# Head of stage 0 in a mixer kernel: v first, a fold in 64x64 quarters, four x tiles ahead of the first softmax, float32 work of PE in shared runs, w1's remainders on GpSimd

## The chip, the cores and the metric

The kernel runs on one core of a Trainium2 chip. The metric is the device time of one execution in microseconds (us), and lower is better. Engines are named as in the profile: PE (TensorE matmul), PEld (its weight loads), DVE (VectorE), ACT (ScalarE), POOL (GpSimd), SP (the queue that issues most transfers).

## The reference

x is 2048 rows of 512. After a layer norm, two branches are added to x: a linear attention with a Hedgehog feature map over 32 heads of 16 (A), and a gated MLP with a spatial 2048x2048 mixing (B). All is float32.

```python
xn = _layernorm(x)
# A
q, k, v = split(xn @ wqkv)                       # 32 heads of 16 each
pq = einsum("bhsd,hdf->bhsf", q, w_phi)          # and pk from k
phi_q = concat([softmax(pq), softmax(-pq)])      # and phi_k from pk
kv = einsum("bhsf,bhsd->bhfd", phi_k, v); z = phi_k.sum(s)
A = (phi_q @ kv) / (phi_q @ z + 1e-6) @ wo
# B
z = gelu(xn @ w_in); z1 = z[..., :688]; z2 = _layernorm(z[..., 688:])
B = (z1 * (w_sp @ z2 + b_sp)) @ w_out
out = x + A + B
```

## The kernel before

**Numbers.** A float32 matrix operand is held as two float32r tiles, a rounded part `h` (made by ACT, `round_h`, L43) and a remainder `l` (`rest_l`, L47, on DVE by default). A product is three float32r matmuls, h by h, h by l, l by h (`mm3`, L51 to L53). Where a matmul's operands are plain float32 (the folds, the transposes, the key-value sums), PE works on float32 directly, and the trace holds two PE records for one such matmul (one for a transpose).

**Stage 0** works on 16 tiles of 128 rows of x. For each tile: load (`fetch`), mean and variance on DVE (`stats`), centring on ACT (`center`) with a negated mean that POOL makes (nm), four 128x128 transposes on PE into `pt`, the split of these into `xT` (h on ACT, l on DVE). Then three projections of 12 matmuls each: k, q and v. The layer norm's 1/std, `r_x`, is applied as a scale when a projection is read. k and q go through `softmax_pair` (two reduces, two subtractions, exp on ACT, a sum, a reciprocal); k's features are then normalised on DVE, added into `zacc` by a transfer that accumulates (POOL's queue), and 16 matmuls of 128 rows by 32 columns add the tile to the key-value sum `kvps` (L273). v is read from PSUM by ACT. For 11 of the tiles z1 = x w1 is projected in stage 0 too (`z1_raw`, two times 12 matmuls `zps` of width 344), and for 5 behind it.

w_phi is folded into the weights of q and k ahead: `fold` (L197) multiplies wq and wk, transposed, with a 512x512 block-diagonal matrix `bd` held as four 128x128 blocks, 16 float32 matmuls for each of the two; the result is split into `wqk_h`, `wqk_l`. wv (`wv_h`, `wv_l`) and w1 are split as they come.

**Order.** Each engine runs its instructions in order. A scheduler in the compiler sets the order from the program's order and its own estimates, with pools that set when a buffer can be used again; `tc.issue_after(i)` puts what is recorded in its block behind `i` on i's engine. The head of stage 0 is written out by hand: `keep` chains each instruction behind those kept before. It begins with 11 idle transposes (`warm_up`), statistics of tile 0, the k fold, k of tile 0, and then v and the rest.

Behind stage 0 come w2's projections with gelu and a second layer norm, the spatial product `g` in a Strassen form (7 products for 8), and the output stage. The change doesn't touch these.

Of the kernel before, what the change touches and what calls it, by code (L numbers as in the profile page):

```python
# [13 lines left out]
ALU = mybir.AluOpType  # L14
# [21 lines left out]
def mixer(ctx: ExitStack, tc: tile.TileContext, x, x_t, wv, wqkT, phi_bd, wo, w_in, wst, b_r, w_out, out):  # L36
# [63 lines left out]
    def softmax_pair(pl, src, tag, scale=1.0, ebufs=2):  # L100

        mm = pl.tile([P, 2, H], F32, tag=tag + "mm", bufs=1, name="mm")
        dve.tensor_reduce(mm[:, 0], heads(src), axis=AX.X, op=ALU.max)
        dve.tensor_reduce(mm[:, 1], heads(src), axis=AX.X, op=ALU.min)
        er = pl.tile([P, NF + 2 * H], F32, tag=tag + "e", bufs=ebufs, name="e")
        e, r = er[:, :NF], er[:, NF:]
        e2 = e.rearrange("p (h a d) -> p h a d", a=2, d=DH)
        dve.tensor_tensor(e2[:, :, 0], heads(src), bc(mm[:, 0], H), op=ALU.subtract)
        dve.tensor_tensor(e2[:, :, 1], bc(mm[:, 1], H), heads(src), op=ALU.subtract)  # L109
# [12 lines left out]
    def zproj(ps, s, w, order=(0, 1)):  # L122

        if ps in (za, kv_ps_p):
            p = [ps.tile([P, D], F32, tag="z", name="zps") for _ in range(2)]
        else:
            q = ps.tile([P, 2, D], F32, tag="z", name="zps")
            p = [q[:, k] for k in range(2)]
        t = xT[s]
        for k, j in enumerate(order):  # L130
            for c in range(ND):
                cs = slice(c * P, (c + 1) * P)
                mm3(p[k][:, :FC], (t[:, 0, cs], t[:, 1, cs]), (w[j][0][:, c], w[j][1][:, c]), c == 0, c == ND - 1)
        return [(slice(k, k + 1), p[k][:, :FC].unsqueeze(1)) for k in range(2)] if ps in (za, kv_ps_p) else [(slice(0, 2), q[:, :, :FC])]
# [6 lines left out]

    LAG = 5
    xT = []
# [17 lines left out]
    with ExitStack() as p0:  # L161
# [16 lines left out]
        def split_w(h, l, src, t):  # L178
            sp.dma_start(t, src)
            round_h(act, h, t)  # L180
            rest_l(l, t, h)

        bd = stage("bd")[:, 0, :D]

        def load_rows(src, x_at={}):
            raw = [stage("wrow") for _ in range(2)]
            parts = [raw[c // 2][:, c % 2, :D] for c in range(ND)]
            for c in range(ND):
                if c in x_at:
                    fetch(x_at[c])  # L190
                sp.dma_start(parts[c], src[c * P:(c + 1) * P, :])
            return parts

        def fold(wT, g, accs):
            gs = slice(g * P, (g + 1) * P)
            for c, acc in accs:
                ins = pe.matmul(acc[:, gs], wT[g][:, c * P:(c + 1) * P], bd[:, gs], start=g == 0, stop=g == NG - 1,  # L197
                                skip_group_check=True).ins
            return ins

        def folded(i, accs, keep=lambda **ins: None):
            for c, acc in accs:
                keep(act=round_h(act, wqk_h[:, i, c], acc))
                keep(dve=rest_l(wqk_l[:, i, c], acc, wqk_h[:, i, c]))

        w1 = [[w1_pool.tile([P, ND, FC], F32R, name=f"w1_{j}{k}") for k in "hl"] for j in range(2)]

        def load_win(dst, j, stp, tag, bufs):
            for c in range(ND):
                t = stp.tile([P, D if tag == "x" else FC], F32, tag=tag, bufs=bufs, name="wst_")  # L210
                split_w(dst[0][:, c], dst[1][:, c], w_in[c * P:(c + 1) * P, j * FC:(j + 1) * FC], t[:, :FC])

        def proj(s, wh, wl):
            p = ps.tile([P, D], F32, tag="mm", name="proj")
            for c in range(ND):
                cs = slice(c * P, (c + 1) * P)
                proj.last = mm3(p, (xT[s][:, 0, cs], xT[s][:, 1, cs]), (wh[:, c], wl[:, c]), c == 0, c == ND - 1)
            return p
# [13 lines left out]
        def stats(s):  # L232
            st6 = wk.tile([P, 6], F32, tag="st6", name="st6")
            dve.bn_stats(st6, xt[s])
            nm = wk.tile([P, 1], F32, tag="nm", name="nm")
            ins = dve.bn_aggr(mv_x[:, s], st6).ins
            pool.tensor_scalar_mul(nm, mv_x[:, s, 0:1], -1.0)
            rstd_of(mv_x[:, s], r_x[:, s:s + 1])
            return nm, ins

        def center(s, nm):
            return act.activation(xt[s], xt[s], AF.Identity, bias=nm).ins
# [8 lines left out]
        def centered(s):  # L251
            center(s, stats(s)[0])
            split_x(transposed(s)[0])

        def proj_v(s):
            v[s] = wk.tile([P, D], F32, tag="v", name="v")
            ins = act.activation(v[s], proj(s, wv_h, wv_l), AF.Copy, scale=r_x[:, s:s + 1]).ins
            return proj.last, ins

        def proj_k(s):  # L260
            return softmax_pair(wk, proj(s, wqk_h[:, 1], wqk_l[:, 1]), "k", r_x[:, s:s + 1])
# [5 lines left out]
        def add_kv(s, er):  # L267
            vs, e = v.pop(s), er[:, :NF]
            dve.tensor_tensor(heads(e), heads(e), bc(er[:, NF:], 2 * H), op=ALU.mult)
            pool.dma_start(zacc, e, accum_op=ALU.add)  # L270
            for m in range(H // 2):
                k = m % 4 * QP
                pe.matmul(kv_acc[k:k + QP, m // 4], vs[:, m * QP:(m + 1) * QP], e[:, m * HP:(m + 1) * HP],  # L273
                          start=s == 0 and m < 4, stop=s == NT - 1, skip_group_check=True)
# [14 lines left out]
        def warm_up(n):  # L289

            t = ps.tile([P, ND, P], F32, tag="mm", name="idle")
            for k in range(n):
                i = pe.transpose(t[:, k % ND], ident, ident).ins
            keep(pe=i)

        with ExitStack() as queue:
# [5 lines left out]
            accs = [(c, (za, kv_ps_p)[c // 2].tile([P, D], F32, tag="z", name="fold")) for c in range(ND)]  # L302
            for g in range(NG):
                if g == NG - 1:
                    pt, i = transposed(0)
                    keep(pe=i)
                keep(pe=fold(wkT, g, accs))
            i, j = split_x(pt)
            keep(act=i, dve=j)
            nm, i = stats(1)  # L310
            keep(dve=i)
# [3 lines left out]
            keep(act=center(1, nm))  # L315
            for c in range(ND):
                keep(act=round_h(act, wv_h[:, c], wvr[c]))
                keep(dve=rest_l(wv_l[:, c], wvr[c], wv_h[:, c]))
            p = proj(0, wqk_h[:, 1], wqk_l[:, 1])
            keep(pe=proj.last)  # L320
            pt, i = transposed(1)
            keep(pe=i)
            i, j = split_x(pt)
            keep(act=i, dve=j)
            nm, i = stats(2)
            keep(dve=i, act=center(2, nm))
            ek = softmax_pair(wk, p, "k", r_x[:, 0:1])
            keep(pe=proj_v(0)[0])
            for k in range(2):
                accs = [(2 * k + m, za.tile([P, D], F32, tag="z", name="fold")) for m in range(2)]  # L330
                for g in range(NG):
                    i = fold(wqT, g, accs)
                folded(0, accs)
                if k == 0:
                    keep(pe=i)
                    pt, i = transposed(2)
                    keep(pe=i)
                    split_x(pt)
                    proj_v(1)
        n1 = nq = 0  # L340
        for s in range(NT):
            fetch(s + 4)
            er = proj_k(s) if s else ek
            if 0 < s < NT - 2:
                centered(s + 2)
            while nq < (s - 2) * NT // (NT - 3):
                proj_q(nq)
                nq += 1
            add_kv(s, er)
            if s + 2 < NT:  # L350
                proj_v(s + 2)
            if s == 1:
                for j in range(2):
                    load_win(w1[j], j, wk, "x", XB)
            while n1 < s * (NT - LAG) // (NT - 1):
                z1_raw(wk, za, n1, 2)
                n1 += 1

# [75 lines left out]
    with ExitStack() as p1:  # L434
# [27 lines left out]
        with ExitStack() as p1a:  # L462
            ta = p1a.enter_context(left("tmp1a", 1))
            for j in range(2):
                load_win(w2[j], 2 + j, ta, "st", 4)
# [407 lines left out]
```

## Time and profile before

| | us |
|---|---|
| median of three runs (lowest, highest) | 646.1 (645.77, 646.1) |
| profiled execution | 645.63 |
| its span, first to last instruction | 643.8 |
| PE busy | 635.9 (99% of the span) |
| PEld busy | 575.6 (89%) |
| DVE busy | 508.5 (79%) |
| ACT busy | 278.4 (43%) |
| POOL busy | 100.3 (16%) |
| mean granted clock of PE | 0.999 of full |

A row of the timeline gives the start in us from the span's start, the busy time, the engine, the line, the operation, what it writes and reads, its shape, the count of merged records, and in brackets the idle time before it and what ended that. Matmuls overlap, so what one costs PE is read from start to start. A row of waits gives the waiting instruction, what it waited for, the total in us, how often, and the longest.

### The profile page before, as it was taken

To read this page: it belongs to the slowest core of one execution; us is meant where nothing else is said; L and a number is where in the kernel's file an instruction comes from. 1 tells how busy PE (TensorE), PEld (TensorE's weight loads), DVE (VectorE), ACT (ScalarE), POOL (GpSimd) and SP (SyncE) were. 2 spreads that over 40 slices of the span, in tenths; PEclk is the share of its full clock that TensorE was granted. 3 is DMA by queue.
4 is the path that set the end of the run, shared out by engine and by line. 5 is a ranking of instruction groups with operands and counts; after the bars stand their busy time and mean duration, and the time that the engine had idled before them with its cause. 6 is when DMAs were issued, how large, how long until landed. Compare 5 with 4: busy or idle time off the path is not lost.

```text
span 643.8 us, 11202 instructions
## 1 busy us (share of the span) xinstructions
PE 635.9 (99%) x4291; PEld 575.6 (89%) x4291; DVE 508.5 (79%) x922; ACT 278.4 (43%) x464; POOL 100.3 (16%) x193
## 2 busy tenths in 40 slices
PE   7999999999999999999999999999999999999997
PEld 6888888888888999999999999999999887888885
DVE  4988887898889669989979678687786598989521
ACT  5653443433333447887534434344343443223330
POOL 3332211201110104452010010100101200001000
PEclk9999999999999999999999999999999999999999
DMA  8265434553463861002452533534458867685620
GB/s 310 73 170 126 115 106 109 148 147 90 125 175 115 263 224 66 2 2 62 135 183 81 170 122 125 173 107 149 121 163 278 293 239 280 231 273 224 221 66 33
DMA packets 38949, 98.12 MB, mean 152 GB/s; under 512 B 4880, under 2 KB 7184, under 8 KB 38896
## 3 DMA queue, kind: packets, MB, share of 16 engines
q1 hardware_dynamic: 27440, 55.99, 27.1%
q0 software_dynamic: 9152, 35.79, 18.5%
q10 hardware_dynamic: 2304, 5.64, 2.3%
q8 instruction: 33, 0.54, 0.3%
q14 instruction: 20, 0.16, 0.1%
HBM read 56.24 MB, written 26.48 MB: 128 GB/s over the span
## 4 chain that ended last, share of the span: by engine, by line
PE 97%; DMA 1%; DVE 1%; ACT 0%; SPq 0%; issue 0%; POOL 0%; POOLq 0%
PE g L53 11%; PE g L52 11%; PE g L51 11%; PE proj L53 7%; PE proj L51 7%; PE proj L52 7%; PE zps L53 6%; PE zps L51 6%; PE zps L52 6%; PE pout L51 6%; PE pout L53 5%; PE pout L52 5%; PE kvps L273 1%; PE ptq L751 1%; PE po L765 1%; PE pt L248 1%
## 5 line engine op out<-in xcount | busy, mean ns | idle before, releaser
L53 PE MATMUL g<-B,A 128*128 128x344 f32 x448 | 143.3, 320 | 0.0
L52 PE MATMUL g<-B,A 128*128 128x344 f32 x448 | 143.2, 320 | 0.0
L51 PE MATMUL g<-B,A 128*128 128x344 f32 x448 | 143.2, 320 | 0.0
L53 PEld LDWEIGHTS g<-B,A 128*128 128x128 f32 x448 | 84.2, 188 | 0.0
L51 PEld LDWEIGHTS g<-B,A 128*128 128x128 f32 x448 | 84.2, 188 | 0.0
L52 PEld LDWEIGHTS g<-B,A 128*128 128x128 f32 x448 | 84.1, 188 | 0.0
L47 DVE TENSOR_TENSOR A<-S,A 128x512 fp32r<-128x512 f32 x64 | 43.8, 689 | 33.5 <-ACT A L43 32.8
L43 ACT ACTIVATE A<-S 128x512 fp32r<-128x512 f32 x64 | 40.1, 631 | 58.6 <-PE g L53 36.0
L110 ACT ACTIVATE e<-e,r_x 128x1024 f32<-128x1024 f32 x32 | 36.8, 1151 | 44.3 <-DVE e L109 43.6
L51 PE MATMUL proj<-wqk_h,xT 128*128 128x512 f32 x128 | 51.4, 401 | 0.3 <-ACT wqk_h L43 0.3
L52 PE MATMUL proj<-wqk_l,xT 128*128 128x512 f32 x128 | 50.5, 394 | 1.1 <-DVE wqk_l L47 1.1
L43 ACT ACTIVATE A<-wf 128x512 fp32r<-128x512 f32 x64 | 33.4, 522 | 41.0 <-PE g L53 39.7
L53 PE MATMUL proj<-wqk_h,xT 128*128 128x512 f32 x128 | 50.9, 397 | 0.0
L51 PE MATMUL zps<-w_0h,xT 128*128 128x344 f32 x128 | 41.8, 326 | 0.0
L112 DVE TENSOR_REDUCE sm<-e 128x64 f32<-128x1024 f32 x32 | 38.7, 1208 | 3.3 <-ACT e L110 3.3
L51 PE MATMUL zps<-w_1h,xT 128*128 128x344 f32 x128 | 41.0, 320 | 0.0
L53 PE MATMUL zps<-w_0h,xT 128*128 128x344 f32 x128 | 41.0, 321 | 0.0
L53 PE MATMUL zps<-w_1h,xT 128*128 128x344 f32 x128 | 41.0, 320 | 0.0
L52 PE MATMUL zps<-w_0l,xT 128*128 128x344 f32 x128 | 40.9, 320 | 0.0
L52 PE MATMUL zps<-w_1l,xT 128*128 128x344 f32 x128 | 40.9, 319 | 0.0
L47 DVE TENSOR_TENSOR A<-wf,A 128x512 fp32r<-128x512 f32 x64 | 35.5, 555 | 3.7 <-ACT A L43 3.3
L51 PE MATMUL pout<-wu,uh 128*128 128x512 f32 x75 | 30.8, 410 | 0.0
(195 smaller groups left out, 1416.3 us busy)
## 6 DMA issues: line engine op xcount, KB each, us to landing
wf<-in_wst SPq DMA_DIRECT2D x64, 256.0 KB, 3.4
e_d<-e POOLq DMA_DIRECT2D x16, 544.0 KB, 5.2
et<-e_d SPq DMA_DIRECT2D x16, 544.0 KB, 5.4
zacc<-e POOLq DMA_DIRECT2D x16, 512.0 KB, 4.9
er<-et POOLq DMA_DIRECT2D x12, 512.0 KB, 4.3
u_d<-z1t POOLq DMA_DIRECT2D x16, 368.0 KB, 4.1
u<-u_d SPq DMA_DIRECT2D x15, 368.0 KB, 5.0
z_d<-z1f ACTq DMA_DIRECT2D x16, 344.0 KB, 3.4
```

The costliest lines, as they stand in the source:

```text
L43: return act.activation(h, src, AF.Copy).ins
L47: return (eng or dve).tensor_tensor(l, src, h.bitcast(F32), op=ALU.subtract).ins
L51: pe.matmul(dst, ah, bh, start=start, stop=False)
L52: pe.matmul(dst, ah, bl, start=False, stop=False)
L53: return pe.matmul(dst, al, bh, start=False, stop=stop).ins
L110: act.activation(e, e, AF.Exp, scale=scale)
L112: dve.tensor_reduce(sm, heads(e), axis=AX.X, op=ALU.add)
L248: ins = pe.transpose(pt[:, c], xs[:, c * P:(c + 1) * P], ident).ins
L273: pe.matmul(kv_acc[k:k + QP, m // 4], vs[:, m * QP:(m + 1) * QP], e[:, m * HP:(m + 1) * HP], start=s == 0 and m < 4, stop=s == NT - 1, ski ...
L751: pe.transpose(pt[:, a, k].bitcast(F32R), src, ident_r)
L765: lasts[3] = pe.matmul(po[r][c * QP:(c + 1) * QP, j // NG], kvT[rows, j], fs[j // 2][rows, j % 2], start=True, stop=True).ins
```

## The change

- v is the first projection: wv is loaded first, its blocks 0 and 2 on ACT's queue and 1 and 3 on SP's behind x0. v and k of tile 0 take the products with the weights' remainders last (`rest_last`).
- The fold uses the fact that `bd` is block-diagonal: it leaves out the 64x64 blocks that are zero and runs 64x64 matmuls, into two PSUM banks, one for each half of the contraction rows. 64 matmuls for k, 32 for each half of q.
- Tiles 0 to 3 are prepared ahead of the first softmax, and tiles 0, 1 and 3 are centred on DVE. The idle work is 7 float32 matmuls of width 256 on a tile of ones.
- From tile 4 on, two tiles' transposes and two tiles' key-value sums stand side by side on PE (`run`, every second tile), behind all that was recorded before. Sums follow their features by one tile more; v has 4 buffers in place of 2, k's features 3 in place of 2.
- w1 is loaded in four pieces of 128x688 in the head, into tiles that later hold xT, and its remainders are made on GpSimd.

PE's order at the start of the program, before (rows of equal instructions are merged, xN is their count; `pt` a tile's transposes, `proj` a projection's PSUM tile):

```order
L293 MATMUL idle<-ident 128x128 x11
L197 MATMUL fold<-bd,wrow 128x128 x12
L248 MATMUL pt<-ident,xt 128x128 x4
L197 MATMUL fold<-bd,wrow 128x128 x4
L51 MATMUL proj<-wqk_h,xT 128x512
L52 MATMUL proj<-wqk_l,xT 128x512
L53 MATMUL proj<-wqk_h,xT 128x512
```

The same place now:

```order
L335 MATMUL idle<-warm 128x256 x6
L268 MATMUL pt<-ident,xt 128x128 x4
L335 MATMUL idle<-warm 128x256
L229 MATMUL proj<-wv_h,xT 128x512 x8
L229 MATMUL proj<-wv_l,xT 128x512 x4
L268 MATMUL pt<-ident,xt 128x128 x4
L206 MATMUL fold<-bd,wrow 64x64 x64
L268 MATMUL pt<-ident,xt 128x128 x4
L51 MATMUL proj<-wv_h,xT 128x512
```

v of tile 0 and the transposes of tile 1 have moved ahead of the k fold, and tile 2's transposes stand right behind it.

PE, the first key-value sum (`kvps`; `zps` is a z1 projection), before:

```order
L51 MATMUL proj<-wv_h,xT 128x512
L52 MATMUL proj<-wv_l,xT 128x512
L53 MATMUL proj<-wv_h,xT 128x512
L248 MATMUL pt<-ident,xt 128x128 x4
L273 MATMUL kvps<-e,v 32x64 x16
L51 MATMUL zps<-w_0h,xT 128x344
L52 MATMUL zps<-w_0l,xT 128x344
```

The same sum now:

```order
L51 MATMUL zps<-w_h,xT 128x344
L52 MATMUL zps<-w_l,xT 128x344
L53 MATMUL zps<-w_h,xT 128x344
L268 MATMUL pt<-ident,xt 128x128 x8
L293 MATMUL kvps<-e,v 32x64 x32
L51 MATMUL proj<-wqk_h,xT 128x512
L52 MATMUL proj<-wqk_l,xT 128x512
```

Two tiles' transposes and two tiles' sums now stand together; before, they stood singly at most places, and next to each other at some.

POOL behind its setup, before (`nm` the negated mean, `r_x` the 1/std of a tile):

```order
L237 TENSOR_SCALAR nm<-mv_x 128x1
L84 TENSOR_SCALAR mv_x<-mv_x 128x1
L85 TENSOR_TENSOR r_x<-mv_x,mhalf 128x1
L270 DMA zacc<-e 128x1024 x2
L237 TENSOR_SCALAR nm<-mv_x 128x1
```

Now:

```order
L254 TENSOR_SCALAR nm<-mv_x 128x1
L84 TENSOR_SCALAR mv_x<-mv_x 128x1
L47 TENSOR_TENSOR w_l<-wrow,w_h 128x688
L85 TENSOR_TENSOR r_x<-mv_x,mhalf 128x1
L47 TENSOR_TENSOR w_l<-wrow,w_h 128x688 x3
L254 TENSOR_SCALAR nm<-mv_x 128x1
L84 TENSOR_SCALAR mv_x<-mv_x 128x1
L286 DMA zacc<-e 128x1024
```

w1's four remainders (`w_l`) stand between the negated means of tiles 4 and 5, ahead of the first zacc transfer.

The diff, cut to what the prediction speaks of:

```diff
         def fold(wT, g, accs):
-            gs = slice(g * P, (g + 1) * P)
-            for c, acc in accs:
-                ins = pe.matmul(acc[:, gs], wT[g][:, c * P:(c + 1) * P], bd[:, gs], start=g == 0, stop=g == NG - 1,
-                                skip_group_check=True).ins
+            for n, banks in accs:
+                for c in range(2):
+                    for m in range(2):
+                        for r in range(2):
+                            rows = slice(r * HP, (r + 1) * HP)
+                            w0, b0 = (2 * n + c) * P + m * HP, g * P + r * HP
+                            ins = pe.matmul(banks[r][m * HP:(m + 1) * HP, c, g], wT[g][rows, w0:w0 + HP],
+                                            bd[rows, b0:b0 + HP], start=g == 0 and c == 0, stop=g == NG - 1,
+                                            skip_group_check=True).ins
             return ins
...
+        def centered_on_dve(s):
+            stats(s)
+            ins = dve.tensor_scalar(xt[s], xt[s], mv_x[:, s, 0:1], None, op0=ALU.subtract).ins
+            rstd_of(mv_x[:, s], r_x[:, s:s + 1])
+            return ins
...
+        def run(tiles, feats):
+            with ExitStack() as order:
+                for i in ahead_of_run:
+                    order.enter_context(tc.issue_after(i))
+                ahead_of_run.clear()
+                pts = []
+                for t in tiles:
+                    pt, i = transposed(t)
+                    pts.append(pt)
+                    order.enter_context(tc.issue_after(i))
+                for t, e in feats:
+                    i = add_kv(t, e)
+            for pt in pts:
+                split_x(pt)
+            return i
+        fetch(0)
+        wvr = load_rows(wv, queues=(act, sp))
+        fetch(1)
         sp.dma_start(bd, phi_bd.rearrange("p g f -> p (g f)"))
-        wkT = load_rows(wqkT[D:], {2: 0})
-        wvr = load_rows(wv, {2: 1})
+        wkT = load_rows(wqkT[D:])
         fetch(2)
         wqT = load_rows(wqkT[:D])
         fetch(3)
+        fetch(4)
+        w1r = load_rows(w_in[:, :FH], FH)
...
         with ExitStack() as queue:
+            warm = wk.tile([P, 2 * P], F32, tag="v", bufs=4, name="warm")
+            keep(dve=dve.memset(warm, 1.0).ins)
...
-            warm_up(11)
-            nm, i = stats(0)
-            keep(dve=i, act=center(0, nm))
+            warm_up(6)
+            keep(dve=centered_on_dve(0))
+            split_v(0)
+            split_v(1)
+            pt, i = transposed(0)
+            keep(pe=i)
+            warm_up(1)
+            split_x_kept(pt)
+            split_v(2)
+            split_v(3)
+            keep(dve=centered_on_dve(1))
+            keep(dve=stats(2))
+            i, j = proj_v(0, True)
+            keep(pe=i, act=j)
+            pt, i = transposed(1)
+            keep(pe=i)
+            split_x_kept(pt)
+            keep(act=center(2))
+            accs = [fold_banks(pl, n) for n, pl in enumerate((za, kv_ps_p))]
             for g in range(NG):
...
                 keep(pe=fold(wkT, g, accs))
             folded(1, accs, keep)
...
+            pt, i = transposed(2)
+            keep(pe=i)
+            split_x_kept(pt)
+            keep(dve=centered_on_dve(3))
+            keep(pe=proj_v(1)[0])
+            p = proj(0, wqk_h[:, 1], wqk_l[:, 1], True)
...
         for s in range(NT):
...
             if s == 1:
-                for j in range(2):
-                    load_win(w1[j], j, wk, "x", XB)
-            while n1 < s * (NT - LAG) // (NT - 1):
+                with tc.issue_after(q_half):
+                    for c in range(ND):
+                        round_h(act, w1_hl[0][:, c], w1r[c])
+                        rest_l(w1_hl[1][:, c], w1r[c], w1_hl[0][:, c], pool)
+            while n1 < (s + 1) * (NT - LAG) // (NT - 1):
                 z1_raw(wk, za, n1, 2)
                 n1 += 1
+            if s and s % 2 == 0:
+                last = run([t for t in (s + 2, s + 3) if t < NT], feats[:-1])
+                behind.close()
+                behind.enter_context(tc.issue_after(last))
+                del feats[:-1]
```

More of the change, by code (lines that the diff above doesn't have):

```diff
@@ L213, in proj @@
[L213 to L217, printed above, removed]
+            for n, banks in accs:
+                h, l = (w[:, i, 2 * n:2 * n + 2].rearrange("p c (g r e) -> p c g r e", g=NG, r=2)
+                        for w in (wqk_h, wqk_l))
+                for r in range(2):
+                    keep(act=round_h(act, h[:, :, :, r], banks[r]))
+                for r in range(2):
+                    keep(dve=rest_l(l[:, :, :, r], banks[r], h[:, :, :, r]))
@@ L340, in mixer @@
         n1 = nq = 0
+        feats, shifted = [], softmax_pair.shifted
+        behind = ExitStack()
         for s in range(NT):
[L342 to L345, printed above, removed]
+            if s:
+                fetch(s + 4)
+            er = ek if s == 0 else softmax_k(s, p1 if s == 1 else proj(s, wqk_h[:, 1], wqk_l[:, 1]))
+            ahead_of_run.append(proj.last)
+            feats.append((s, normalise(er)))
+            if 0 < s < NT - 1:
+                ahead_of_run.append(proj_v(s + 1)[0])
+            if 0 < s < NT - 3:
+                with tc.issue_after(shifted):
+                    stats(s + 3)
+                center(s + 3)
+                shifted = softmax_pair.shifted
```

132 lines of the change are left out of this document (65 added, 67 removed).

## The prediction

> **What bounds the kernel now.** I read the page's busy line and its chain first, then the waits of PE, then PE's timeline through the head, and then the few rows of the other engines that feed the head.
>
> ```profile
> PE 635.9 (99%) x4291; PEld 575.6 (89%) x4291; DVE 508.5 (79%) x922; ACT 278.4 (43%) x464; POOL 100.3 (16%) x193
> PE 97%; DMA 1%; DVE 1%; ACT 0%; SPq 0%; issue 0%; POOL 0%; POOLq 0%
> PE idle L293 <- POOL ident masks.py:199: 1.8, 1, 1.8
> PE proj L52 <- DVE wqk_l L47: 1.1, 1, 1.1
> PE fold L197 <- DMA wrow<-in_wqkT: 0.5, 2, 0.3
> PE proj L51 <- ACT wqk_h L43: 0.3, 1, 0.3
> PE pt L248 <- ACT xt L242: 0.2, 1, 0.2
> ```
>
> PE is busy for 99% of the span, 97% of the chain is PE, and all its waits add up to 3.9 us. So the time falls by what is taken from PE's own work or from the head, and by nothing else, as long as no new wait of PE appears. The head, from PE's timeline (start, busy, then what ended an idle gap):
>
> ```profile
> 1.81 2.61 PE L293 MATMUL idle<-ident 128*128 128x128 f32 x11 [1.81 <-POOL ident masks.py:199]
> 4.22 1.44 PE L197 MATMUL fold<-bd,wrow 128*128 128x128 f32 x8
> ...
> 10.51 0.49 PE L51 MATMUL proj<-wqk_h,xT 128*128 128x512 f32 x1 [0.28 <-ACT wqk_h L43]
> 12.14 0.50 PE L52 MATMUL proj<-wqk_l,xT 128*128 128x512 f32 x1 [1.14 <-DVE wqk_l L47]
> 12.71 0.40 PE L51 MATMUL proj<-wqk_h,xT 128*128 128x512 f32 x1
> 12.95 0.39 PE L52 MATMUL proj<-wqk_l,xT 128*128 128x512 f32 x1
> ...
> 14.78 0.60 PE L248 MATMUL pt<-ident,xt 128*128 128x128 f32 x4
> 15.14 0.47 PE L51 MATMUL proj<-wv_h,xT 128*128 128x512 f32 x1
> 15.45 0.39 PE L52 MATMUL proj<-wv_l,xT 128*128 128x512 f32 x1
> ```
>
> From 12.71 us PE never waits again. By then it has done the k fold (32 matmul records), one tile's transposes and three projection matmuls. The unit costs are start-to-start: a projection matmul 0.23 us (12.71 to 12.95), a whole projection 12 x 0.23 = 2.78; a tile's transposes 0.35 (14.78 to 15.14), and the first matmul behind them is 0.08 late (0.31 instead of 0.23), so 0.43 in all.
>
> **Part by part.** (a) The runs and the fold need these rows of PE.
>
> ```profile
> 18.00 1.95 PE L197 MATMUL fold<-bd,wrow 128*128 128x128 f32 x16
> 20.02 0.66 PE L248 MATMUL pt<-ident,xt 128*128 128x128 f32 x4
> ...
> 26.52 1.95 PE L197 MATMUL fold<-bd,wrow 128*128 128x128 f32 x16
> 28.22 0.47 PE L53 MATMUL proj<-wv_h,xT 128*128 128x512 f32 x1
> 28.53 0.39 PE L51 MATMUL proj<-wv_h,xT 128*128 128x512 f32 x1
> ...
> 30.59 0.60 PE L248 MATMUL pt<-ident,xt 128*128 128x128 f32 x4
> 31.12 0.65 PE L273 MATMUL kvps<-e,v 128*32 128x64 f32 x32
> ...
> 51.19 0.40 PE L53 MATMUL proj<-wqk_h,xT 128*128 128x512 f32 x1
> 51.52 0.65 PE L273 MATMUL kvps<-e,v 128*32 128x64 f32 x32
> 52.10 0.51 PE L51 MATMUL proj<-wv_h,xT 128*128 128x512 f32 x1
> 52.45 0.39 PE L52 MATMUL proj<-wv_l,xT 128*128 128x512 f32 x1
> ...
> 513.36 1.09 PE L765 MATMUL po<-f,kvT 64*32 64x256 f32 x32
> 514.39 0.54 PE L640 MATMUL ptu<-zb,u 128*128 128x128 f32 x4
> ```
>
> A tile's key-value sum (kvps) starts 0.33 after the matmul ahead of it, 0.10 more than that matmul's 0.23; lasts 0.58 (51.52 to 52.10); and the matmul behind it is 0.12 late: 0.80. Transposes right ahead of it take 0.53 instead of 0.35 (30.59 to 31.12), so today's chance neighbours gain nothing: the price is one of changing the tile shape, not of leaving float32r. Two tiles today: 2 x (0.43 + 0.80) = 2.46. One shared run: transposes 0.70, change 0.18, sums 2 x 0.58, end 0.12: 2.16. Six pairs save 6 x 0.30 = 1.8; tiles 12 and 13, which share a run without transposes, 0.22; tile 3's transposes now lie against a fold, 0.08. **Runs: -2.1 us.**
>
> (b) The fold. Each half of q's 4 weight blocks is 16 records today, 2.02 (18.00 to 20.02) and 1.70 (26.52 to 28.22) plus 0.08 behind it: 3.80. The changed kernel issues 32 matmuls of 64x64 per half, 64 records if a float32 matmul is two records there too (16 kvps matmuls are 32 records). No row has that shape. Lower bound: a 128-column record takes 1.70/16 = 0.106, so 64 columns 0.053, four quarters side by side 0.013 each. That row halves run side by side is borne out by po (64x32 tiles, 256 columns): 32 records in 1.03 us, 0.032 each, where 256 columns alone last 0.21. Nearest row: kvps, also 64 columns and four tiles, 0.58/32 = 0.018. Upper bound: a transpose, one record with 128 columns of weights, takes 0.35/4 = 0.088; if weights are loaded one after another, 64 columns cost half of it, 0.044. I take kvps's 0.018, the same moving width and tile count: 1.16 a half. With changes of shape (0.18 + 0.10 behind transposes, 0.10 + 0.12 between projections) q costs 2.82. **q fold: -1.0 us**; ends -1.6 (0.013) and +2.3 (0.044). The k fold becomes 128 records, 2.32, and enters (c).
>
> The Trainium skill ("TensorE: Matmul & The Clock Gate", section LDWEIGHTS) prices a weight load at its columns divided by 1.2, in ns: 53 for 64 columns. Taken one after another, 256 loads would be 13.7 us instead of my 4.6, and the sum would be +4.8 instead of -4.3. The trace speaks against this as a serial price, since kvps's 32-column records follow each other in 0.018 where the rule gives 0.027.
>
> (c) The head. Loads and the engines' rows:
>
> ```profile
> bd<-in_phi_bd SPq DMA_DIRECT2D x1, 256.0 KB, 2.6
> 2.17 4.42 DMA xt<-in_x
> 5.78 0.33 SPq L191 DMA_DIRECT2D wrow<-in_wv  x1
> 7.25 2.35 SPq L191 DMA_DIRECT2D wrow<-in_wqkT  x4
> 6.62 0.69 DVE L234 BATCH_NORM_STATS2 st<-xt 128x6 f32<-128x512 f32 x1 [6.62 <-DMA xt<-in_x]
> 7.34 0.18 DVE L236 BATCH_NORM_AGGREGATE mv_x<-st 128x2 f32<-128x6 f32 x1
> 13.80 2.49 DVE L47 TENSOR_TENSOR wv_l<-wrow,wv_h 128x512 fp32r<-128x512 f32 x4
> 9.37 0.60 ACT L43 ACTIVATE xT<-pt 128x512 fp32r<-128x512 f32 x1 [0.75 <-PE pt L248]
> 12.56 2.18 ACT L43 ACTIVATE wv_h<-wrow 128x512 fp32r<-128x512 f32 x4
> 3.67 0.46 POOL L154 TENSOR_TENSOR mask<-mask 128x128 f32<-128x128 f32 x1
> zacc<-e POOLq DMA_DIRECT2D x16, 512.0 KB, 4.9
> ```
>
> The first 256 KB lands at 3.4 (0.80 + 2.6), the fourth at 6.59. Eight loads are in flight, and each later one is issued when the load eight before it lands: the 11th issue at 5.78 gives the third landing, the four issues of the 7.25 row, 0.67 apart, the fifth to eighth. So 256 KB lands every 0.67 from 6.6 on. The new order is x0 on SP beside the first block of wv on ACT, then two wv blocks, one wv block, x1, bd, four blocks of wk, x2. By position x0 lands at 3.4 to 5.8; I take 4.1. The second and third wv blocks land between 5.8 and 6.6, the fourth at 7.3, x1 at 7.9, the last of wk at 11.3, x2 at 12.0.
>
> - x0: statistics 0.72, aggregate 0.20, centring on DVE at most 0.69 (no row; a 128x512 operation of DVE takes that, a lower end is 0.3): 5.75. Transposes follow; ACT can round xT 0.69 after their start (8.68 to 9.37 today), 6.5.
> - ACT takes wv's second block first, from 6.2 (middle) for 0.55; xT to 7.4; wv's third and fourth to 8.5. PE's last h-by-h matmul goes at 8.5. DVE goes through its five remainders at 0.62 each, the last at about 9.4, and PE ends v of tile 0 near 10.6.
> - x1 now waits for DVE: 9.4 + 0.72 + 0.20 + 0.69 = 11.0; transposes 0.35, change 0.18; the k fold starts at 11.6 (ends 11.3 and 12.2, by the landing of the wv blocks and the centring), behind all its loads.
> - Then x2's centring ends at 14.0 (landing 12.0, 0.72, 0.20, nm 0.35, ACT 0.73), when the fold ends at 13.9. The remainders of wk, 4 x 0.62 behind ACT's rounding, are done near 17; k of tile 0 reads them from 11.6 + 2.42 + 0.43 + 2.78 + 1.85 = 19.1. No wait.
>
> From there PE runs. Beside the old 12.71: later start -1.1; nine more projection matmuls done -2.1; one more set of transposes done -0.4; the k fold still to do, +2.3 and 0.1 for leaving it. **Head: -1.2 us.** Of it the k fold alone is some -1.1 (32 x 0.106 = 3.4 today); the rest of the head ends where it ended.
>
> (d) Costed at nothing, with the cover named. DVE loses w1's eight remainders and gains three centrings; it is not the bound. ACT issues two loads (0.4 each by SP's rows) before its table load, both done before x0 lands. SP's queue has four 344 KB loads for w1 in place of eight later ones, landing near 20, and x5 behind them. w1's four remainders on GpSimd, 128x688: DVE and PE orders put them between the statistics of tile 4 (about 25.4) and the first zps, which PE reaches at 34.3 and whose last block it needs at 35.8. Each may take 2.46 us. The one such GpSimd row, 128x128, took 0.46: in proportion 2.46, and with a fixed part of 0.2 about 1.6. I take 1.6. If the cover is gone, each 0.1 us more costs PE 0.4, ACT's centring of x5 stands behind it in both queues, and tile 0's zacc transfer in GpSimd's, which nothing reads before pz. At the stage's end the last zacc transfer (4.9 after issue) lands about when PE reaches pz: 0, up to 1.5.
>
> **Sum:** -2.1 - 1.0 - 1.2 = -4.3. The profiled execution took 645.63 and would take 641.3; the median of the runs shown, 646.1, is 0.5 above it, so 641.8.
>
> **Rivals.** (A) Weights set the pace of the 64x64 fold, one load after another: 256 x (0.044 - 0.018) = +6.7, so 646.1 - 4.3 + 6.7 = 648.5, slower. It decides from 0.035 us a record. For: a transpose's 0.088 for 128 columns is above its 0.053 of streaming. Against: neighbours in the new order use different row halves, and kvps shows 0.018 with full rows. (B) The head is worse: wv lands with the sixth load or the first matmuls run at the start's pace (0.22 for an idle transpose against 0.088), and the fold starts at 13.2: 643.4. (C) GpSimd takes 3.5 us for each remainder beside a busy DVE: PE waits 4.2, 646.0, no change. (D) Half of (A), 0.030 to 0.040 a record: 645.0 to 647.4, about no change.
>
> The Trainium skill ("GPSIMD Engine Reference", section Performance versus the Vector engine) gives 4497 ns for 2048 float32 columns of such an operation; by it, 688 would be an estimated 1.5 us, and (C) needs the sharing of ports that its Key points name.
>
> **How the numbers follow.** Forecast 0.68, B 0.16, C 0.06, D 0.04, A 0.06. The forecast's own range is 639.8 (record 0.013, early head) to 643.5 (late head, a wait at pz). The whole range reaches over B and to the near edge of C and D: 639.8 to 644.9, which leaves out A and most of C and D. 0.2% (1.3 us) is about what a measurement can tell from no change: faster 0.84 (forecast and B), same 0.10 (C, D), slower 0.06 (A).
>
> **What would show it.** Right: fold rows of 64x64 near 0.018 us a record; six runs of eight transposes and 32 kvps matmuls with one change inside; fold of k starting at 11.3 to 12.2; PE's waits all before 14 us and its busy time some 3 us lower. Wrong: 64x64 records at 0.035 or more, a wait of zps on POOL, of pz on DMA or of pt on ACT, or a k fold that starts after 13.

## The result, and the profile after

The changed kernel takes 642.94 us in the median of four runs (642.76 to 643.11), where the kernel before took 646.1 beside it: the ratio is 0.9947, with a 95% interval of 0.9929 to 0.9964. Six later runs of it gave 643.19. The forecast was 641.8. The profiled execution took 643.11 where the sum said 641.3; its span fell by 2.4, from 643.8 to 641.4.

PE's share of the busy line and of the chain on the page of the changed kernel:

```profile
PE 634.0 (99%) x4486; PEld 575.2 (90%) x4486; DVE 507.7 (79%) x918; ACT 273.8 (43%) x457; POOL 105.5 (16%) x194
PE 96%; DVE 3%; ACT 0%; POOL 0%; issue 0%
```

PE is still the bound, but its busy time fell by 1.9 and not by some 3, and the chain now has 3% of DVE in it. The waits of PE say where to look:

```profile
PE zps L51 <- ACT z1f L140: 1.8, 1, 1.8
...
```

The waits of the old head (1.1 for a remainder, 0.5 for loads) are gone, and one of 1.8 is new: a z1 product (`zps`) waits until ACT has read an earlier one from PSUM (`z1f`). It stands far behind the head, as PE's timeline shows:

```profile
1.24 5.49 PE L335 MATMUL idle<-warm 128*128 128x256 f32 x12 [1.24 <-DVE warm L348]
6.53 1.02 PE L268 MATMUL pt<-ident,xt 128*128 128x128 f32 x4
...
8.24 2.47 PE L229 MATMUL proj<-wv_h,xT 128*128 128x512 f32 x8 [0.25 <-ACT xT L43]
...
12.16 2.10 PE L206 MATMUL fold<-bd,wrow 64*64 64x64 f32 x128
14.19 0.66 PE L268 MATMUL pt<-ident,xt 128*128 128x128 f32 x4
...
27.81 1.16 PE L206 MATMUL fold<-bd,wrow 64*64 64x64 f32 x64
28.91 0.51 PE L52 MATMUL proj<-wqk_l,xT 128*128 128x512 f32 x1
...
39.80 0.32 PE L53 MATMUL zps<-w_h,xT 128*128 128x344 f32 x1
41.89 0.43 PE L51 MATMUL zps<-w_h,xT 128*128 128x344 f32 x1 [1.77 <-ACT z1f L140]
...
43.88 1.04 PE L268 MATMUL pt<-ident,xt 128*128 128x128 f32 x8
44.85 1.10 PE L293 MATMUL kvps<-e,v 128*32 128x64 f32 x64
45.88 0.50 PE L51 MATMUL proj<-wqk_h,xT 128*128 128x512 f32 x1
46.22 0.39 PE L52 MATMUL proj<-wqk_l,xT 128*128 128x512 f32 x1
```

From start to start, the k fold takes 2.03 (128 records, 0.016 each), the second half of q 1.10 (64 records, 0.017 each), and the first shared run 0.97 + 1.03 with 0.10 behind it, 2.10. Behind the matmul at 39.80 PE has the next z1 product to begin and no PSUM tile for it until ACT's z1f is done. Why ACT is late is read from POOL's timeline and ACT's. POOL:

```profile
25.43 1.69 POOL L47 TENSOR_TENSOR w_l<-wrow,w_h 128x688 fp32r<-128x688 f32 x1
...
27.61 5.93 POOL L47 TENSOR_TENSOR w_l<-wrow,w_h 128x688 fp32r<-128x688 f32 x3
...
34.10 1.06 POOL L286 DMA_DIRECT2D zacc<-e  x1
...
39.43 0.90 POOL L286 DMA_DIRECT2D zacc<-e  x1 [3.63 <-ACT e L110]
40.41 0.24 POOL L254 TENSOR_SCALAR nm<-mv_x 128x1 f32<-128x1 f32 x1
```

ACT:

```profile
40.68 0.72 ACT L256 ACTIVATE xt<-xt,nm 128x512 f32<-128x512 f32 x1 [1.24 <-POOL nm L254]
41.31 0.53 ACT L140 ACTIVATE z1f<-zps,r_x 128x344 f32<-128x344 f32 x1
```

w1's remainders hold POOL until 33.5, while DVE has tile 0's features ready at 32.0. Tile 0's zacc transfer goes at 34.10 and, at the 4.7 from issue to landing that the trace gives for it, lands near 38.8. Tile 1's adds to the same accumulator and waits for that: 39.43. The row names ACT's exponential as what ended this wait, but that ended at the same moment by chance: experiment 1's row names the transfer, and in experiment 2 the second transfer goes before the exponential ends. From one transfer to the next it is 5.3 in all three. The negated mean of tile 6, a 0.24 us operation whose statistics were ready at 39.1, stands behind it in POOL's queue: 40.41. ACT idles 1.24 for it, centres tile 6 at 40.68, and only then reads the z1 product that PE waits for, at 41.31. This was a reading of the trace; the experiments test it.

### The profile page after: what moved, and what is told of

Read it like the earlier page. It is cut to its first block, busy times and chain, and to the rows that moved or that the text cites. A ratio compares the mean times of both kernels' runs of the same rounds, so it can differ in the third digit from the quotient of the medians.

```text
span 641.4 us, 11562 instructions
## 1 busy us (share of the span) xinstructions
PE 634.0 (99%) x4486; PEld 575.2 (90%) x4486; DVE 507.7 (79%) x918; ACT 273.8 (43%) x457; POOL 105.5 (16%) x194
## 4 chain that ended last, share of the span: by engine, by line
PE 96%; DVE 3%; ACT 0%; POOL 0%; issue 0%
PE g L53 11%; PE g L52 11%; PE g L51 11%; PE proj L51 6%; PE zps L51 6%; PE proj L53 6%; PE proj L52 6%; PE zps L53 6%; PE zps L52 6%; PE pout L51 6%; PE pout L52 5%; PE pout L53 5%; PE ptq L826 1%; PE po L840 1%; PE kvps L293 1%; PE pout L854 1%
## 5 line engine op out<-in xcount | busy, mean ns | idle before, releaser
L112 DVE TENSOR_REDUCE sm<-e 128x64 f32<-128x1024 f32 x32 | 38.8, 1212 | 14.4 <-ACT e L110 14.3
L51 PE MATMUL proj<-wqk_h,xT 128*128 128x512 f32 x124 | 49.5, 400 | 0.0
L52 PE MATMUL proj<-wqk_l,xT 128*128 128x512 f32 x124 | 48.7, 393 | 0.0
L53 PE MATMUL proj<-wqk_h,xT 128*128 128x512 f32 x124 | 48.7, 393 | 0.0
L51 PE MATMUL zps<-w_h,xT 128*128 128x344 f32 x128 | 41.8, 327 | 1.8 <-ACT z1f L140 1.8
L53 PE MATMUL zps<-w_h,xT 128*128 128x344 f32 x128 | 40.9, 320 | 0.0
L52 PE MATMUL zps<-w_l,xT 128*128 128x344 f32 x128 | 40.8, 319 | 0.0
L140 ACT ACTIVATE z1f<-zps,r_x 128x344 f32<-128x344 f32 (+1 forms) x29 | 16.5, 575 | 34.5 <-PE zps L53 32.4
L828 ACT ACTIVATE f<-ptq 128x512 f32<-128x512 f32 x32 | 16.5, 603 | 32.2 <-PE ptq L826 25.8
L694 POOL DMA_DIRECT2D u_d<-z1t x16 | 8.7, 545 | 131.0 <-DVE A L47 107.2
```

The costliest lines, as they stand in the source:

```text
L51: pe.matmul(dst, ah, bh, start=start, stop=False)
L52: pe.matmul(dst, ah, bl, start=False, stop=False)
L53: return pe.matmul(dst, al, bh, start=False, stop=stop).ins
L140: act.activation(z[:, k], p, AF.Copy, scale=r_x[:, s:s + 1])
L694: pool.dma_start(u_d[2 * i + k], z[:, k])
L828: act.activation(f, pt.rearrange("p a k b -> p a (k b)"), AF.Copy)
```

## The experiments

All times are medians of four to twelve runs, with the interval of the ratio to the kernel before. Each edit is to the changed kernel, or to the experiment named.

**1. w1's remainders on DVE again.**

```diff
-                        rest_l(w1_hl[1][:, c], w1r[c], w1_hl[0][:, c], pool)
+                        rest_l(w1_hl[1][:, c], w1r[c], w1_hl[0][:, c])
```

> The changed kernel, with w1's four remainders (128x688) on DVE again; PE's order stays as it is. The changed kernel has one new wait of PE, 1.8 us at 40 us, for ACT's z1f. Theory 1 (GpSimd's queue): the remainders hold GpSimd until 33.5, so tile 0's zacc transfer is issued at 34.1 and lands at 38.9, tile 1's, which must wait for it, goes at 39.4, the negated mean of tile 6 behind it at 40.4, ACT's centring behind that and z1f behind the centring. Without the remainders GpSimd issues tile 0's transfer some 3 us earlier and the wait of 1.8 is gone: 641.1 (641.0 to 641.4). Rival (DVE's lateness): DVE ends tile 0's softmax late and holds ACT's exponential; with four more operations of about 0.8 us it is later still, and the wait stays at 1.8 or reaches 4: 643 to 645. Rival (another wait takes its place): zps waits for DVE or ACT in the same place, 642.5 to 643.2.

642.26 (0.9929 to 0.9953). The wait was halved, not gone, so no theory had it whole. Its waits, its second zacc transfer and its ACT:

```profile
PE zps L51 <- ACT z1f L140: 0.9, 1, 0.9
```

```profile
40.99 0.87 POOL L286 DMA_DIRECT2D zacc<-e  x1 [4.26 <-DMA zacc<-e]
```

```profile
38.60 1.15 ACT L110 ACTIVATE e<-e,r_x 128x1024 f32<-128x1024 f32 x1 [2.10 <-DVE e L109]
```

Theory 1 was wrong in a step of its own: tile 0's transfer did not go earlier but at 35.65, since DVE, with w1 on it, normalised tile 0 later (until 34.7). So this run does not test whether the remainders delay the transfer. The scheduler also put the centring behind z1f in ACT's queue, where it holds nothing up. What is left is the rival of DVE's lateness: DVE, with four operations more, ends its subtraction late, the exponential waits 2.10 for it, and z1f stands right behind the exponential, at 39.66.

**2. The negated mean on DVE, w1 left on GpSimd.**

```diff
-            pool.tensor_scalar_mul(nm, mv_x[:, s, 0:1], -1.0)
+            dve.tensor_scalar_mul(nm, mv_x[:, s, 0:1], -1.0)
```

> The changed kernel, with the negated mean of each tile made on DVE behind its aggregate instead of on GpSimd; w1's remainders stay on GpSimd. So ACT's centring no longer stands behind GpSimd's queue, while the zacc transfers stay as late as they are. Theory 1 (what reaches PE is the negated mean in GpSimd's queue): the wait of PE for z1f near 40 us is gone or under 0.3, 641.1 to 641.5. Rival (the late zacc transfers or the slow remainders reach PE another way, by the exponential or the reuse of buffers): the wait stays at 1.5 or more, 642.6 to 643.2. Rival (16 small operations more on DVE delay its remainders): no change or up to 0.5 slower.

641.78 (0.9918 to 0.9944). POOL, ACT and the waits of PE:

```profile
25.11 7.57 POOL L47 TENSOR_TENSOR w_l<-wrow,w_h 128x688 fp32r<-128x688 f32 x4
...
32.81 1.05 POOL L286 DMA_DIRECT2D zacc<-e  x1
...
38.12 0.91 POOL L286 DMA_DIRECT2D zacc<-e  x1 [3.64 <-DVE st L249]
```

```profile
38.53 0.71 ACT L256 ACTIVATE xt<-xt,nm 128x512 f32<-128x512 f32 x1
39.15 0.53 ACT L140 ACTIVATE z1f<-zps,r_x 128x344 f32<-128x344 f32 x1
```

```profile
PE zps L51 <- ACT z1f L140: 0.2, 1, 0.2
```

The remainders are as slow as before (7.57 for four), the second zacc transfer goes as late as before behind the first (5.31 after it), and the wait is 0.2. ACT's order is that of the changed kernel, with the exponential (37.48 to 38.63) ahead of the centring. So neither the remainders nor the late transfers reach PE by themselves: what reached it was the small operation queued behind them. In this execution the k fold also began at 11.26, 0.90 earlier than in the changed kernel's profile; experiment 5 shows why, and that the wait comes earlier by as much.

**3. Three warm-up matmuls instead of six** (`warm_up(3)`).

> The changed kernel with three warm-up matmuls ahead of tile 0's transposes instead of six. Tile 0 is centred at 5.43, and its transposes start at 6.53, behind six matmuls of 0.44 us. Theory: the transposes start at 5.5, about 1 us earlier, or less if the clock, full from 7.39, comes later for want of matmuls; the k fold starts 0.3 to 0.6 earlier than 12.16. Since the wait of 1.8 at 40 us ends when GpSimd and ACT are done and not when PE arrives, it grows by what the head gains: 2.1 to 2.4, and the time stays at 642.8 to 643.1. Rival (the wait moves with PE): 642.3 to 642.6. Rival (fewer warm-ups leave the clock low for longer): the fold starts at 12.2 or later, 643 to 643.5.

643.17 (0.9949 to 0.9971), the same. Tile 0's transposes came 0.69 earlier, and the last rival was right. PE's timeline, and the stretch behind its wait (its length, then the busy time of PE, PEld, DVE, ACT and POOL with counts in brackets, then PE's granted clock, the DMA share and GB/s):

```profile
5.84 0.63 PE L268 MATMUL pt<-ident,xt 128*128 128x128 f32 x4 [1.67 <-POOL mv_x L84]
...
7.16 3.54 PE L229 MATMUL proj<-wv_h,xT 128*128 128x512 f32 x8 [0.25 <-ACT xT L43]
```

```profile
7.50:11.00 3.50, 3.50 (x10) 2.52 (x9) 2.80 (x6) 0.64 (x2) 0.98 (x2) 0.51 1.05 397
```

PE idled 1.67, and from 7.5 on ran 3.4 us at half clock: the eight matmuls took 3.54 instead of 2.47, which ate the gain, and the k fold began at 12.16 again.

**4. The old fold of 128x128 blocks, for k and q** (`fold`, `folded` and the PSUM tiles as in the kernel before).

> The changed kernel with the fold of 128x128 blocks of the kernel before, for k and for q; the rest is as changed. By PE's rows the k fold takes 3.4 (32 records of 0.106) instead of 2.03, and each half of q 1.70 plus 0.08 instead of 1.09 plus changes of shape of 0.2: 1.35 and 2 x 0.5 to 0.6, together 2.4 to 2.6 more work of PE. Theory 1 (the wait for z1f ends by GpSimd's and ACT's queues, not by PE's arrival): PE arrives 2.5 later, the wait of 1.8 is gone, and the time rises by 0.6 to 0.8 only: 643.6 to 643.8. Rival (the wait moves with PE): 645.4 to 645.6, with 1.8 left at z1f. Rival (the 64x64 fold brings nothing): 642.9 or less.

644.57 (0.9959 to 0.9981): 1.6 slower than the changed kernel (1.4 against its later runs), between the two theories. PE's timeline and waits, and its ACT:

```profile
11.84 3.74 PE L198 MATMUL fold<-bd,wrow 128*128 128x128 f32 x32
15.42 0.60 PE L255 MATMUL pt<-ident,xt 128*128 128x128 f32 x4
...
21.83 1.95 PE L198 MATMUL fold<-bd,wrow 128*128 128x128 f32 x16
23.54 0.47 PE L51 MATMUL proj<-wqk_h,xT 128*128 128x512 f32 x1
```

```profile
PE pz L507 <- DMA zacc<-e: 0.5, 1, 0.5
...
PE g L53 <- DVE A L47: 0.2, 1, 0.2
```

```profile
40.48 0.55 ACT L140 ACTIVATE z1f<-zps,r_x 128x344 f32<-128x344 f32 x1 [0.30 <-PE zps L53]
...
42.35 0.72 ACT L243 ACTIVATE xt<-xt,nm 128x512 f32<-128x512 f32 x1 [1.32 <-POOL nm L241]
```

The k fold is 3.58, 1.55 more than 2.03, and a half of q 0.50 more, 2.55 in all as priced. The wait for z1f is gone, but not for theory 1's reason, that PE arrives later: in this program the scheduler put z1f ahead of the centring, which still waits 1.32 for its negated mean. New are the waits at pz (the product that reads zacc behind stage 0) and at the spatial product g, 0.7 together. So the 1.6 is the price of the fold less a wait that the new order removed, and not of the fold alone; experiment 11 is the cleaner test.

**5. The changed kernel again.**

> The changed kernel again, unchanged, beside the next three. The clock record of the runs so far begins its full speed between 5.6 and 7.4 us of the span where the start of the program is the same, and the k fold then starts between 11.3 and 12.2. Theory (the start's pace differs from execution to execution, by when the full clock is granted): the k fold starts within 11.2 to 12.2, the wait of PE for z1f ends near 41.9 wherever the fold started, so that an early head only makes the wait longer (1.8 plus what the head gains), and the time is 642.7 to 643.2. Rival (the wait follows PE): an early head makes the time shorter by as much, 642.0 to 642.4.

643.19 (0.9937 to 0.9965). Both answers were wrong in part. The k fold began at 11.16 and the wait ended at 40.92, both 1.0 earlier than in the first profile, so the wait does move with the head; yet the profiled execution was not faster, 643.75. Its PE, and the stretch behind the wait with the granted clock (columns as in experiment 3):

```profile
1.24 4.41 PE L335 MATMUL idle<-warm 128*128 128x256 f32 x12 [1.24 <-DVE warm L348]
...
40.92 0.42 PE L51 MATMUL zps<-w_h,xT 128*128 128x344 f32 x1 [1.74 <-ACT z1f L140]
...
43.70 1.86 PE L268 MATMUL pt<-ident,xt 128*128 128x128 f32 x8
45.49 1.10 PE L293 MATMUL kvps<-e,v 128*32 128x64 f32 x64
```

```profile
42.00:45.40 3.40, 3.40 (x15) 3.14 (x14) 0.00 (x0) 1.14 (x2) 0.94 (x1) 0.50 0.49 147
```

The same twelve warm-up records took 4.41 here and 5.49 there, which moves the head by 1.0. And here the wait of 1.7 was followed by 3.4 us at half clock: eight transposes took 1.79 instead of 0.97. In the changed kernel's first profile the same stretch has a clock of 1.00. From the start of the k fold to pz this execution needed 1.64 more, with the same waits. The other executions agree: the two of the six with a mean clock of 0.997 took 643.75 and 644.50, the four at 1.00 took 642.21 to 643.22. So a wait of this length costs its own 1.8, and in some executions up to 1.7 more.

**6. Both edits, negated mean and w1 on DVE.**

> Both edits: the negated mean on DVE, and w1's remainders on DVE. With w1 alone on DVE a wait of 0.9 for z1f was left. Theory A (there it came from DVE: the exponential waited for DVE's subtraction, and z1f stands behind the exponential): it stays at 0.6 to 1.2, and the time is 642.0 to 642.5, slower than with the negated mean alone on DVE (641.8). Theory B (there too it was ACT's centring behind GpSimd's queue): the wait is under 0.3 and the time 641.5 to 641.8.

642.58 (0.9932 to 0.9956), with 0.8 of the wait left: theory A by the size of the wait, but not by its mechanism. Here z1f (38.26) stands behind a centring and ahead of the exponential (39.23):

```profile
37.63 0.72 ACT L256 ACTIVATE xt<-xt,nm 128x512 f32<-128x512 f32 x1 [2.62 <-DVE nm L254]
```

DVE had the mean at 34.1 and made the negated mean at 37.46, behind a normalisation and three reduces. So with w1 on DVE it is DVE's queue that is late, and the small operation is stuck there instead. By the medians GpSimd is the better place for the remainders once nothing small stands behind them (641.78 against 642.58), though single runs of the two overlap.

**7. No shared runs, on experiment 2** (each tile's transposes and its `add_kv` recorded by themselves, `run` left out).

> The negated mean on DVE, and each tile's transposes and key-value sum placed by themselves as in the kernel before, so without shared runs. By the rows measured, a pair of tiles in a shared run adds 2.10 to the projections around it; alone they add 2 x (0.43 + 0.80) = 2.46, and the two sums of tiles 12 and 13 1.58 instead of 1.23. Theory (a change of tile shape has a price each time): 6 x 0.36 + 0.35 = 2.5 slower than the 641.8 with runs, 0.3 to 0.5 less where transposes happen to lie against other float32 work: 643.8 to 644.3. Rival (the runs bring nothing, since single sums hide between projections): 641.6 to 642.2. Rival (the free order brings a new wait in stage 0): over 644.5, with PE's waits showing it.

643.92 (0.9955 to 0.9978), 2.1 slower than with runs (641.78). A sum that stands alone, in its PE:

```profile
44.25 0.40 PE L51 MATMUL proj<-wqk_h,xT 128*128 128x512 f32 x1
44.57 0.65 PE L293 MATMUL kvps<-e,v 128*32 128x64 f32 x32
45.16 0.50 PE L52 MATMUL proj<-wqk_l,xT 128*128 128x512 f32 x1
45.50 0.39 PE L53 MATMUL proj<-wqk_h,xT 128*128 128x512 f32 x1
```

The sum stands 0.32 behind the matmul ahead of it, takes 0.59, and the next matmul needs 0.34 instead of 0.23: 0.79, as in the kernel before (0.80); a lone set of transposes costs 0.43. The profiled execution, 645.16, is the slowest of the six. From the start of the k fold to pz it needs 2.7 more than experiment 2's, 0.3 of it a wait at pz; behind pz it loses 1.9 more, with waits of 0.6 and 0.4 at g. How much of that the faster executions have is not known, so the 2.1 is not all shown to be the price of the changes of shape.

**8. Five warm-up matmuls, on experiment 2.**

> The negated mean on DVE, and five warm-up matmuls instead of six. Tile 0 is centred at 5.4 to 5.8, while six matmuls keep PE until 6.05 (clock early) or 6.53 (clock late). Theory: the transposes start at 5.6 to 5.9, the gap after the warm-ups is under 0.3 so that the clock is not lowered again, and the k fold starts 0.2 to 0.6 earlier at the same clock: 641.2 to 641.6 against 641.8. Rival (the clock is lowered again, as with three warm-ups, where a gap of 1.7 was followed by 3.4 us at half clock): the fold starts at 12.0 or later and the time is 642.2 or more. Rival (another operation of the head, DVE's remainders of wv, sets the fold's start): no change, 641.7 to 641.9.

641.31 (0.9910 to 0.9934), 0.5 below experiment 2, whose runs overlap with these. The gap behind the warm-ups was 0.34, no half clock followed, and the k fold began at 10.88. A part came back as a wait for tile 2:

```profile
PE pt L268 <- ACT xt L256: 0.6, 1, 0.6
```

**9. The same, with tile 2's negated mean left on GpSimd.**

```diff
-            dve.tensor_scalar_mul(nm, mv_x[:, s, 0:1], -1.0)
+            (pool if s == 2 else dve).tensor_scalar_mul(nm, mv_x[:, s, 0:1], -1.0)
```

> Five warm-up matmuls, and the negated mean on DVE for all tiles but the third, for which it stays on GpSimd. With five warm-ups and the negated mean always on DVE, PE waited 0.6 us at 12.9 for the centring of tile 2: DVE made its negated mean at 12.62, behind a remainder, while GpSimd, idle there, made it 0.27 behind the aggregate in the changed kernel. Theory: the transposes of tile 2 start 0.3 to 0.6 earlier and all that follows with them, 640.7 to 641.1 against 641.3. Rival (the gain comes back as a wait for z1f near 40): 641.2 to 641.5.

640.83 (0.9905 to 0.9932), in the theory's range, and the fastest here: 2.1 below the changed kernel, 5.1 below the one before (645.98 beside it). The step from 641.31 alone is smaller than the runs can tell apart; in its profile the wait for tile 2 fell from 0.6 to 0.2, but its transposes start only 0.19 earlier (13.38), since the fold began later there (11.12).

**10. The head with k first, on experiment 8** (bd and wk loaded ahead of x1 and wv, the k fold behind tile 0's transposes, k of tile 0 ahead of v).

> As with five warm-ups and the negated mean on DVE (641.3), but the head the other way round: bd and the four blocks of wk are loaded ahead of x1 and wv, PE folds k behind tile 0's transposes and projects k of tile 0 ahead of v. So it undoes 'v first' alone; the fold, the runs and the tiles prepared ahead stay. By the landings and rows measured the fold starts near 7.2 and ends at 9.3, ACT rounds its four parts by 11.4, k of tile 0 ends at 13.2, ACT and DVE split wv until 14.3 and 15.3, and v of tile 0 ends at 15.6, where v first has the same work done at 13.57 + 2.78 = 16.35. Theory A (v first brings nothing of its own; the head's work fits in either order): 640.6 to 641.6. Theory B (v first is what keeps PE fed, as its split needs no fold): PE waits 1 us or more for wqk's rounding or for wv, 642.0 to 643.5.

644.61 (0.9969 to 0.9987), 3.3 slower than experiment 8: above both theories, and mostly not for theory B's reason. PE's timeline and waits:

```profile
16.91 0.66 PE L268 MATMUL pt<-ident,xt 128*128 128x128 f32 x4 [0.51 <-ACT xt L256]
...
20.97 1.16 PE L206 MATMUL fold<-bd,wrow 64*64 64x64 f32 x64
```

```profile
PE zps L51 <- ACT z1f L140: 1.7, 1, 1.7
...
PE zps L51 <- DVE e L109: 0.9, 1, 0.9
```

The k fold began at 7.06. At the first half of q's fold both orders have done the same work: this one gets there at 20.97, v first at 20.13 in experiment 8's profile. So the head itself is 0.8 worse, with small waits of 0.3 and 0.2 for the second centring and for wqk's rounding and one of 0.5 at tile 2 (experiment 8 has one of 0.6 there). The larger loss is 2.6 of waits near 40, where experiment 8 has 0.2: there DVE and ACT fell behind. Which of the moved operations delays them was not separated.

**11. The old fold, on experiment 2.**

> The negated mean on DVE (641.8), with the fold of 128x128 blocks. On the changed kernel itself the old fold put 2.55 us of work back (k 3.58 instead of 2.03, each half of q 0.50 more), but the time rose by 1.6 only, since the wait of 1.8 for z1f was gone with it and 0.5 of a wait for the last zacc transfer came. With no such wait left to fill, theory: 641.8 + 2.55 - 0.2 = 644.1, up to 0.5 more by a wait at pz: 643.9 to 644.6. Rival (the fold is worth less than its rows, since PE waits for other things in its place): 643.4 or less.

643.77 (0.9951 to 0.9978), 2.0 slower than experiment 2: just under the theory's low end of 643.9, and above the rival's 643.4. There was hardly a z1f wait to lose here (0.2); a wait of 0.6 at pz is in it. That it comes out above experiment 4's 1.6 is within what the runs can tell.

## Why the prediction was right, and where it was not

**The run and fold prices, (a) and (b): right, and a little too cautious.** A shared run measured 2.10 against 2.16. What stands of transposes and sums between the projections sums to 18.5 us of PE in the trace before (tiles 3 to 15's transposes, all sums) and to 15.9 in the trace after: -2.6 where the sum said -2.1, and experiment 7 gives back 2.1. The 64x64 record was 0.016 to 0.017 where 0.018 was taken; q's halves cost 1.37 and 1.29 with their changes of shape, 2.66 against 2.82 priced. Rival A, serial weight loads, is out: the trace has a record every 16 to 17 ns, where A needed 44 and decided from 35. The Trainium skill ("TensorE: Matmul & The Clock Gate", section LDWEIGHTS) gives 53 ns for a load of 64 columns; taken one after another, such loads would not fit in the measured pace.

**The head, (c): right in size, late at its start.** The k fold began at 12.16, at the late end given; in the profiles of experiments 1, 2, 4 to 7 and 11, with the same first instructions, it began at 10.95 to 11.84. The step that was mis-sized is "5.75" for tile 0's transposes: they began at 6.53, since six warm-up matmuls at the start's pace outlasted the centring of x0, which ended at 5.4. The sum has no term for the warm-up matmuls; its own terms also give 5.71, not 5.75. The k fold itself was 2.03 and not 2.32, which gave 0.3 back of the 0.6 by which its start missed 11.6.

**At nothing, (d): the step that failed.** The remainders took 1.69 and 1.98, within the 2.46 that their direct reader allowed, and zps did not wait for them. What failed is the sentence that tile 0's zacc transfer stands behind them, "which nothing reads before pz". It is not read, but the next transfer on the queue waits for it, and behind that one stand the negated means that ACT needs. Here the queue, not the data, made ACT depend on the transfer. Experiment 2 takes exactly this link away, and the wait falls from 1.8 to 0.2. The link ahead of it, that the remainders made the first transfer late, is read from the trace alone (features ready at 32.0, transfer at 34.10, remainders until 33.5): experiment 1 was to test it and could not. The other cover named there, ACT's centring, was indeed what waited, but at tile 6 and not at tile 5. So the sign that all of PE's waits come before 14 us did not hold.

**The sum.** Up to the start of pz the profiled executions differ by 2.8: runs -2.6, q -1.1, the wait with its restart +1.9, which leaves -1.0 for the head (priced -1.2). Behind pz 0.4 was lost without a wait of PE: that part took 426.5 before and 426.9 in the changed kernel and in experiments 2, 3, 5 and 8, and no run explains it. The median came within 1.2 of the forecast, and the profiled execution within 1.8 of the sum, in part by luck: runs and q came out 0.6 better than priced, against the 1.9 that was missed. Rival C had the right engine with the wrong price (3.5 a remainder): it came true as a queue. The 1.5 allowed at pz did not come in the changed kernel. The ends of the forecast's range do not follow from the terms given: 0.013 a record and a fold 0.3 earlier make 640.2 and not 639.8, a fold 0.6 later and 1.5 at pz make 643.9 and not 643.5.

## What to carry to other kernels

When work is moved onto an engine with time to spare, go through everything that stands behind it in that engine's queue, not only through its readers: a transfer that must wait for the one before it turns a delay that nobody reads into a stop for each small operation behind. Then ask which of those small operations another engine waits for, and move that one; here it was cheaper to move than the work itself. When you move something to test a reading, compare the other engines' order too: in experiments 1, 4 and 6 the scheduler changed ACT's order, and with it the wait. Price a wait of PE like the ones of 1.7 to 1.8 us here at up to twice its length, since the clock can be halved after it. Don't fill the start with more warm-up than the first operand needs, nor with so little that a long gap opens.

## What the hardware showed that was not expected

- **Half clock after a gap.** Gaps of PE of 1.67 and 1.74 us were followed by 3.4 us at a granted clock of 0.50 to 0.51 (experiments 3 and 5), beginning 1.7 and 1.0 us after the gap's end. The gaps of 1.77 in the changed kernel's first profile, 1.78 in experiment 3 and 1.69 in experiment 10, all near 40, were not, and one of 0.34 was not. The Trainium skill ("TensorE: Matmul & The Clock Gate", section Part 1: The HAM clock gate) describes a free-running window of 3413 ns by whose activity the clock is set. The length agrees, and a window that runs freely would explain why the same gap costs 1.64 more in one execution than in another; that is not shown here. By the same section the clock falls after a whole window without work, and here gaps of half that length were enough, so on that point the measurement decides.
- **DVE beside GpSimd.** The normalisation of 128x1024, with both inputs in SBUF, took 2.05 while GpSimd made w1's remainders, and 1.21 once it had ended; with w1 on DVE it took 1.19 (experiment 1). The changed kernel's DVE:

```profile
29.95 2.05 DVE L285 TENSOR_TENSOR e<-e 128x1024 f32<-128x1024 f32 x1
...
35.85 1.21 DVE L285 TENSOR_TENSOR e<-e 128x1024 f32<-128x1024 f32 x1
```

- **The start's pace varies.** The same twelve warm-up records took 4.32 to 5.49 us in different executions, and the k fold, between 10.95 and 12.16, moved with them.
